# Keys of the first chunk transposed by TensorE instead of by DMA, with new stage priorities, in a two-layer attention and MLP kernel

## Chip, cores, metric

The kernel runs on one core of a Trainium2 chip. The metric is the device time of one execution in microseconds (us). An execution is called fast unless it fell in a slower state of the chip (lower TensorE clock throughout); all comparisons here are of fast runs. Engine names as in the profile: PE is TensorE (PEld its weight loads), ACT ScalarE, DVE VectorE, POOL GpSimd, SP SyncE, which issues most DMAs.

## The reference

Two layers over a sequence of 2048 rows of width 576: sliding-window attention, then an MLP, each behind a layer norm and with a residual.

```python
def _A_ref(x, wqkv, wo):                       # B, S, D = 1, 2048, 576
    H = 32; Dh = 18; W = 256
    q, k, v = ...  # (x @ wqkv) split into three and into heads
    scores = einsum("bhqd,bhkd->bhqk", q, k) * Dh ** -0.5
    mask = (i - j >= 0) & (i - j < W)
    p = softmax(where(mask, scores, -1e9))
    return (p @ v, heads joined) @ wo
def _B_ref(x, w1, b1, w2, b2):                 # inner width 4608
    return gelu(layernorm(x) @ w1 + b1) @ w2 + b2
x = A_x
for layer in range(2):                         # written out in the original
    x = x + _A_ref(layernorm(x), A_wqkv, A_wo)
    x = x + _B_ref(layernorm(x), B_w1, B_b1, B_w2, B_b2)
```

## The kernel before

The rows of each layer are cut into four chunks of 512, so there are eight chunks, 0 to 7. Attention of one chunk runs beside the MLP of the chunk before: ACT's exponentials leave PE time, and the matmuls of the second MLP product (hT times w2) fill it. I call those matmuls *filler*. A chunk's attention has 24 units (one group of four heads times one set of key blocks), in two stages of twelve (`ea`, `eb`); a unit is one group of score matmuls, two exponentials on ACT, masks on POOL, and 16 small matmuls with the values. The MLP of a chunk runs in two halves (`ga`, `gb`).

The order of instructions isn't written by hand. Each piece of work is a task with an estimated duration and a priority, and a planner places them one at a time, by the earliest possible start and then by priority:

```python
class Plan:
    def add(self, eng, fn, ..., cost=0.1, lat=0.1, prio=0.0, ...):
        stage = self.stage + ("+" if dma in ("w1", "w2", "xr") else "")
        prio += self.nudge.get(stage, 0.0)       # the annealed shift of this stage
        ...
    def schedule(self):
        ...
                    key = (round(st, 3), t.prio, t.idx)   # st: earliest start by the plan's costs
```

In the first 140 us the planner also puts warm-up matmuls into holes that it foresees on PE. The priorities, `PL.nudge`, hold one shift for each stage and were found by annealing, a search that changes them at random and mostly keeps what helps.

The queries and keys of a chunk come out of the projection as rows in PSUM, are cast to bf16 by DVE and ACT (`qn`), and have to be transposed, since the scores contract over the head dimension. Before, DMA did it, eight 128x128 blocks at a time:

```python
def qkv(k, i, prio0):                            # chunk k, row block i
    for n, w in enumerate("qkv"):
        bs = two_out(...)                        # projection on PE into two PSUM banks
        ...                                      # casts into qn by DVE and ACT
        dst, dn = ...                            # where the transposed block goes: qT or kT
        add("sp", lambda e, dst=dst, sl=sl: e.dma_start_transpose(dst, qn[:, sl, :]),
            reads=[f"qn{sl}h0", f"qn{sl}h1"], writes=[dn], dma="t", ...)
```

The softmax here doesn't subtract the row's maximum and nothing guards it: scores larger than these inputs give would overflow.

## Time and profile before

| | before |
|---|---|
| median of three runs | 934.0 us (932.31 to 935.26) |
| span of the profiled run | 932.2 us, mean PE clock 0.996 |
| PE busy | 900.0 us, 97% |
| PE idle from 0 to 100 us | 14.3 us |
| PE idle from 800 to 820 us | 3.25 us, clock 0.83 |

The prediction shows the lines behind this table. PE's matmuls of the MLP begin, in each half, with a group of six whose weights have 64 rows (a line reads `64*128 64x512`). The starts of the first such group of each half are good marks for comparing two kernels: 16 halves, the first at 100.1 us, then 149.6, and the last three at 764.5 (`ga` of chunk 6), 813.2 (`gb` of chunk 6) and 855.5 (`ga` of chunk 7), before a last half at 891.4. A half clock shows in the windows view at a fine grain. Its columns are the stretch, its length, busy time of PE, PEld, DVE, ACT and POOL, then the granted PE clock as a share of the full one, and two columns for DMA (its busy share and GB/s) that the argument doesn't use.

### The profile page before, as it was taken

What the parts mean: (1) busy time and instruction counts of PE and PEld (TensorE: products, weight loads), DVE (VectorE), ACT (ScalarE), POOL (GpSimd) and SP (SyncE); (2) the same over time, 40 slices, a digit from 0 to 9 for tenths busy, and PEclk for the clock granted to TensorE, in tenths of its full rate; (3) what the DMA queues carried; (4) which work ended last, traced back from release to release, by engine and by line L of the source; (5) the groups of instructions that cost most, each with busy time, mean ns of one, the idle gap of its engine ahead of it and who ended that gap; (6) DMA issues with size and microseconds to landing.
All of it is one profiled execution on the core that took longest, in us unless ns stands there. A gap on an engine that the chain in (4) does not pass through costs nothing. (4 is left out here: it accounts for less than half of the span.)

```text
span 932.2 us, 22378 instructions
## 1 busy us (share of the span) xinstructions
PE 900.0 (97%) x9343; PEld 566.3 (61%) x9382; DVE 320.0 (34%) x796; ACT 593.9 (64%) x717; POOL 372.8 (40%) x507
## 2 busy tenths in 40 slices
PE   8888999999999999999999999999999999899998
PEld 6555465655756657566565647577475665647556
DVE  5746222452238322174221812275022610232001
ACT  3687677767735777564677668636776677752541
POOL 3777444453504635054241635125452453500100
PEclk9999999999999999999999999999999999999999
DMA  9997839564295332964348351873619534345430
GB/s 212 137 248 123 201 95 259 130 156 124 47 242 118 116 115 28 240 139 140 113 66 253 66 191 40 215 147 63 198 39 234 137 119 144 113 121 148 160 115 26
DMA packets 225684, 130.06 MB, mean 140 GB/s; under 512 B 156080, under 2 KB 223408, under 8 KB 225584
## 3 DMA queue, kind: packets, MB, share of 16 engines
q1 hardware_dynamic: 216272, 120.95, 53.0%
q0 software_dynamic: 6880, 5.03, 4.1%
q10 hardware_dynamic: 2432, 2.65, 0.9%
q8 instruction: 74, 1.21, 0.6%
q14 instruction: 26, 0.21, 0.1%
HBM read 91.87 MB, written 2.36 MB: 101 GB/s over the span
## 5 line engine op out<-in xcount | busy, mean ns | idle before, releaser
L749 ACT ACTIVATE pT<-ps 128x1024 bf16<-128x1024 f32 (+2 forms) x384 | 347.9, 971 | 134.5 <-PE ps L740 133.2
L770 POOL TENSOR_SCALAR_AFFINE_SELECT pT<-pT 128x512 bf16<-128x512 bf16 (+1 forms) x368 | 282.0, 790 | 268.9 <-ACT pT L749 260.5
L904 PE MATMUL ps<-w_sb,hT 128*128 128x288 bf16 x2304 | 314.9, 286 | 1.3 <-DVE x_res L821 1.0
L878 ACT ACTIVATE hT<-ps,b1col 128x512 bf16<-128x512 f32 x288 | 198.0, 688 | 169.6 <-PE ps L875 169.6
L875 PE MATMUL ps<-xnTm,w_sb 128*128 128x512 bf16 x1113 | 259.4, 381 | 2.9 <-issue 1.2
L904 PEld LDWEIGHTS ps<-w_sb,hT 128*128 128x128 bf16 x2304 | 210.9, 97 | 73.5 <-issue 19.1
L875 PEld LDWEIGHTS ps<-xnTm,w_sb 128*128 128x128 bf16 x1152 | 109.4, 98 | 134.0 <-issue 17.7
L821 DVE TENSOR_TENSOR x_res<-ps,x_res 128x288 f32<-128x288 f32 x160 | 71.5, 449 | 244.5 <-PE ps L904 217.8
L670 PE MATMUL ps<-wqkv,xnTa 128*128 128x288 bf16 x960 | 135.8, 286 | 7.0 <-DVE qn L705 4.8
L670 PEld LDWEIGHTS ps<-wqkv,xnTa 128*128 128x128 bf16 x960 | 88.1, 98 | 44.4 <-DVE qn L705 10.0
L787 PEld LDWEIGHTS ps<-vA,pT 128*128 128x128 bf16 x2880 | 94.4, 96 | 27.5 <-POOL pT L770 11.0
L787 PE MATMUL ps<-vA,pT 128*128 128x20 bf16 x2880 | 100.7, 172 | 4.6 <-DVE attq L802 2.8
L705 DVE CAST qn<-ps 128x288 bf16<-128x288 f32 x120 | 54.5, 456 | 143.6 <-PE ps L670 141.1
L886 POOL TENSOR_TENSOR x_res<-x_res,b2bc 128x576 f32<-128x576 f32 x32 | 44.9, 1402 | 97.3 <-ACT hT L878 97.3
L740 PE MATMUL ps<-qT,kT 32*128 32x384 bf16 (+2 forms) x1216 | 64.1, 276 | 5.0 <-ACT pT L749 3.0
L602 POOL TENSOR_SCALAR vtmp<-mv_all 128x1 f32<-128x1 f32 (+1 forms) x43 | 8.4, 195 | 126.9 <-DVE mv_all L593 125.4
L591 DVE BATCH_NORM_STATS2 st_all<-x_res 128x6 f32<-128x288 f32 x104 | 44.6, 446 | 7.8 <-DMA x_res<-in_A_x_dram 6.6
L670 PE MATMUL ps<-wo_sb,attT 128*128 128x288 bf16 x320 | 45.4, 286 | 1.7 <-DVE x_res L821 1.7
L692 DVE CAST vA<-ps 128x288 bf16<-128x288 f32 x64 | 28.9, 454 | 50.6 <-PE ps L670 50.5
L863 PE MATMUL ps<-xnTm,w_sb 64*128 64x512 bf16 x288 | 40.2, 382 | 3.1 <-ACT pT L749 2.2
L797 DVE RECIPROCAL rinv<-ps 128x16 f32<-128x16 f32 x64 | 16.3, 255 | 76.6 <-PE ps L787 76.4
L740 PEld LDWEIGHTS ps<-qT,kT 32*128 32x128 bf16 x1216 | 19.5, 92 | 33.5 <-issue 19.2
(39 smaller groups left out, 290.9 us busy)
## 6 DMA issues: line engine op xcount, KB each, us to landing
w_sb<-in_B_w_dram SPq DMA_DIRECT2D x48, 864.0 KB, 6.2
w_sb<-in_B_w_dram SPq DMA_DIRECT2D x48, 768.0 KB, 4.8
w_sb<-in_B_w_dram SPq DMA_DIRECT2D x96, 48.0 KB, 4.5
x_res<-in_A_x_dram POOLq DMA_DIRECT2D x4, 1152.0 KB, 8.1
out_dram<-xn SPq DMA_DIRECT2D x16, 144.0 KB, 1.9
wqkv<-in_A_wqkv_dram ACTq DMA_DIRECT2D x3, 576.0 KB, 6.8
hT<-in_A_x_dram SPq DMA_DIRECT2D x2, 576.0 KB, 6.4
wo_sb<-in_A_wo_dram ACTq DMA_DIRECT2D x1, 576.0 KB, 6.6
```

The lines of the kernel that those rows point to most:

```text
L591: add("dve", lambda e, i=i, s=s: e.bn_stats(st_all[:, t, i, :], s[:, t, i * HB:(i + 1) * HB]), reads=res, writes=[f"st{t}_{i}"], cost=0.37 ...
L670: ins = e.matmul(bank(bs[o])[:, 0:HB], lhs(c), rhs(c, o * HB), start=(c == 0), stop=(c == KD - 1))
L705: add("dve", lambda e, b=bs[o], dst=dst: e.tensor_copy(dst, bank(b)[:, 0:HB].rearrange("p (h d) -> p h d", d=DH)), reads=[bs[o]], writes=[ ...
L740: ins = e.matmul(two(bs[j // 2])[:, j % 2, col:col + nq * 128], k_of(T0 + so)[0][32 * j:32 * j + 32, g, :], qs[32 * j:32 * j + 32, g, qo * ...
L749: add("act", lambda e, h2=h2: e.activation(pT[:, sl, 2 * h2:2 * h2 + 2, lo:hi], two(bs[h2])[:, :, lo:hi], ACT.Exp, scale=SCALE), reads=[bs ...
L770: add("pool", lambda e, ap=ap, pat=pat, sgn=sgn, kind=kind: e.affine_select(ap, ap, pattern=pat, compare_op=(ALU.is_ge if kind == "d" else ...
L787: ins = e.matmul(bank(B_O)[:, o:o + VW], pT[:, sl, j, col + qi * 128:col + (qi + 1) * 128], vA[:, (T0 + so) % VS, 4 * g + j, :], start=(fi ...
L821: add("dve", lambda e: e.tensor_tensor(x_res[:, t, sl], bank(b)[:, 0:HB], x_res[:, t, sl], ALU.add), reads=[b], writes=[f"x{t}h{hh}"], cos ...
L875: ins = e.matmul(bank(bk)[:, 0:n], w1_sb[:, sl, col:col + 128], xnTm[:, k % 2, c, 0:n], start=False, stop=(c == 3))
L878: add("act", lambda e, ff=ff, fl=fl, bk=bk: e.activation(hT[:, fl, 0:n], bank(bk)[:, 0:n], ACT.Gelu_apprx_tanh, bias=b1col[:, ff:ff + 1]), ...
L886: add("pool", lambda e, t=t: e.tensor_tensor(x_res[:, t, :], x_res[:, t, :], b2bc[:, :], ALU.add), reads=["b2", f"h{fl}"], writes=X(t), co ...
L904: ins = e.matmul(bank(b)[:, 0:HB], hT[:, fl, i * 128:(i + 1) * 128], w2_sb[:, fl, hh * HB:(hh + 1) * HB], start=(fl == 0), stop=(fl == NFH ...
```

## The change

The intent: keys of the first chunk should not wait in the DMA queue, where seven of the eight transposes of the chunk leave one after another behind a load of input rows. For the keys of chunk 0 alone, PE transposes the eight blocks into a PSUM bank and ACT copies the bank out. Since this shifts the load of each engine, the priorities were annealed again.

```diff
-    PL.nudge = {"ea0": -16.73, "q1.0": -5.72, "q1.1": -31.53, ...        # 53 stages
+    PL.nudge = {"": 0.63, "ld0+": 7.4, "q1.0": -16.88, "q1.1": 0.39, ... # 44 stages, none with the old value
...
+                if k == 0 and (w == "k"):
+                    b = Bank(FILL)
+                    def fn(e, b=b, sl=sl):
+                        ins = None
+                        for c in range(G):                                # G = 8
+                            ins = e.transpose(bank(b).bitcast(BF16)[:, c * 128:(c + 1) * 128],
+                                              qn[:, sl, c * 128:(c + 1) * 128], ident[:, :])
+                        return ins
+                    add("pe", fn, ..., cost=0.55, lat=0.22, prio=prio - 0.02, alloc=[b])
+                    src = bank_of(b)
+                    add("act", lambda e, dst=dst, src=src: e.copy(dst, src()), ..., cost=0.95, lat=0.17, prio=prio)
+                    continue
                 add("sp", lambda e, dst=dst, sl=sl: e.dma_start_transpose(dst, qn[:, sl, :]), ...
```

## The prediction

> **What bounds the kernel now.** I read the page's share of each engine first, then the list of engine busy times in 20 us windows, the chain of waits that ended last, and the timeline of the two stretches where the windows show TensorE (PE) idle.
>
> The page, engine totals:
> ```profile
> PE 900.0 (97%) x9343; PEld 566.3 (61%) x9382; DVE 320.0 (34%) x796; ACT 593.9 (64%) x717; POOL 372.8 (40%) x507
> ...
> PE 40%; DVE 2%; ACT 1%; issue 0%; DMA 0%; POOL 0%; DVEq 0%; POOLq 0%
> ```
> PE is busy 900.0 of 932.2 us, and the chain that ended last is PE work for nearly all that it could follow; DMA and ScalarE (ACT) have about 1% or less of it. So a change pays only by (a) taking away PE work, (b) taking away some of the 932.2 - 900.0 = 32.2 us of PE idle, or (c) taking away time in which PE ran at a lower clock. Windows (length, then busy PE, PEld, DVE, ACT, POOL, then the granted clock and DMA):
> ```profile
> 0.00:20.00 20.00, 17.66 (x135) 13.50 (x135) 10.61 (x30) 6.56 (x12) 7.54 (x23) 1.00 0.91 214
> 20.00:40.00 20.00, 16.40 (x207) 11.05 (x207) 14.39 (x44) 11.81 (x17) 11.86 (x16) 1.00 1.83 148
> 40.00:60.00 20.00, 16.70 (x246) 10.69 (x247) 10.89 (x27) 15.91 (x23) 15.53 (x23) 1.00 1.26 238
> 60.00:80.00 20.00, 17.01 (x285) 10.65 (x282) 8.04 (x20) 18.91 (x23) 15.44 (x21) 1.00 1.04 174
> 80.00:100.00 20.00, 17.97 (x271) 12.82 (x271) 16.74 (x45) 12.41 (x14) 12.98 (x23) 1.00 0.74 117
> 100.00:120.00 20.00, 19.68 (x115) 9.13 (x118) 1.17 (x3) 13.41 (x20) 6.22 (x6) 1.00 0.78 232
> ...
> 800.00:820.00 20.00, 16.75 (x221) 10.40 (x220) 3.45 (x9) 13.34 (x15) 9.53 (x13) 0.83 0.44 141
> ```
> The first 100 us hold 100 - 85.74 = 14.3 us of PE idle; the window at 800 holds 3.25 us more and is the only one in mid-kernel whose clock is under 1.00. From 100 to 800 the idle sums to about 11 us in 700. So there are two places to gain anything: the start, where chunk 0's keys are made, and one gap near 810.
>
> **The start.** Timeline of the kernel before (start, length, engine, line, what; in brackets the idle before it and its releaser):
> ```profile
> 13.17 3.60 SPq L712 DMA_TRANSPOSE kT<-qn  x1
> ...
> 18.79 1.18 DVE L591 BATCH_NORM_STATS2 st_all<-hT 128x6 f32<-128x288 bf16 x3 [1.63 <-DMA hT<-in_A_x_dram]
> ...
> 20.38 1.40 PE L670 MATMUL ps<-wqkv,xnTa 128*128 128x288 bf16 x10 [1.27 <-DVE qn L705]
> ...
> 22.14 0.34 PE L740 MATMUL ps<-qT,kT 32*128 32x384 bf16 x4 [0.36 <-DMA qT<-qn]
> ...
> 27.54 0.40 PE L740 MATMUL ps<-qT,kT 32*128 32x384 bf16 x8 [0.98 <-DMA kT<-qn]
> ...
> 27.98 4.39 ACT L749 ACTIVATE pT<-ps 128x1024 bf16<-128x1024 f32 x6 [3.94 <-PE ps L740]
> ```
> Eight DMA transposes (four of queries, four of keys) leave one queue in turn. The issue of the first key transpose takes 3.60 us, since a load of input rows stands before it. The first scores start at 22.14, the second, which need keys 1 and 3, only at 27.54, behind a key transpose. ACT idles 3.94 us for them. After that ACT runs the exponentials of chunk 0 and the first of chunk 1 until 80.1 with further waits of 1.26, 0.85, 2.36, 0.30, 0.38, 1.04, 0.75 and 0.24 us (7.2 in sum): this stretch goes at ACT's pace, not PE's.
>
> **The gap near 810.**
> ```profile
> 810.36 0.40 PE L740 MATMUL ps<-qT,kT 32*128 32x256 bf16 x8 [1.13 <-ACT pT L749]
> ...
> 813.20 1.46 PE L863 MATMUL ps<-xnTm,w_sb 64*128 64x512 bf16 x6 [1.89 <-ACT pT L749]
> ```
> At the end of the last attention chunk PE has run out of other matmuls: it waits 1.13 and 1.89 us for exponentials. The six matmuls then take 1.46 us where the same six take 0.82 elsewhere: half clock. The stretch from 813 to 819 has a mean clock of 0.53.
>
> **What the Trainium skill says.**
> 1. "TensorE: Matmul & The Clock Gate", Part 4: PE-mode transpose, gives about 275 ns for a 128x128 transpose within a kernel and says that the result lands in PSUM and has to be copied out. Five such transposes are in this trace (line L628): 219 ns each, but pipelined, ten in 0.89 us, so 0.089 us apiece.
> 2. "VectorE: DVE Perf Modes", The three transpose paths, gives 1309 ns for the DMA transpose of one 128x128 block. The key transposes here carry eight blocks, hold the queue for a median of 1.28 us and land after a median of 3.3 us, up to 9.4. So latency, not throughput, is what the change can remove.
> 3. "ScalarE: Activation LUTs", What ACT_TABLE_LOAD costs: 186 ns + 0.833 ns per element with immediate scale and bias, which for 1024 elements is 1.04 us. The trace agrees: exponentials over 1024 elements take 1025 ns and the copies of 640 elements 694 (formula: 719).
> 4. "TensorE: Matmul & The Clock Gate", Why this matters for your kernels, warns of PE idle gaps of more than about 3 us because of the clock. Here 1.13 + 1.89 us, parted by one short group, were followed by the half clock, so the trace agrees roughly.
>
> **The change, part by part.**
> *Removed:* four DMA transposes from the queue, at least 4 x 1.28 = 5.1 us of issue time between 13 and 26 us, and the latency of keys. The three later query transposes move up. Also three of 50 warm-up matmuls, 0.3 us.
> *Added on PE:* 4 x 8 transposes x 0.089 = 2.85 us, all before the second scores. PE is idle 1.27 + 0.36 + 0.98 us and more in that stretch, so they fit in idle time; if the exponentials still set the pace until 80 us, this costs nothing.
> *Added on ACT:* four copies of 1024 elements, about 0.97 each pipelined = 3.9 us. The order of instructions of the changed kernel puts two before the first exponential, where ACT idles 0.7 to 0.8 us between its casts, and two between the first and second unit, in the place of the 3.94 us wait. So not free, but hidden.
> *First scores:* they need queries 0 to 2. In the kernel before, queries 1 and 2 held the queue from 16.87 to 19.90; with the first key gone, query 1 takes the stalled slot (ends about 17), query 2 ends about 18.5. They could land 1.5 us earlier. But the changed order has VectorE (DVE) start the row statistics after the fifth cast, not the sixth. In the kernel before those statistics waited 1.63 us for the input rows, till 18.79, holding up the next cast. That wait now stands before the cast of query 3, so PE gets its next PSUM bank about 20.1, and the first scores come about 20.9: 1.2 us gained.
> *Second scores:* DVE has then statistics between the casts of keys 2 and 3; I add 1.4 us of them, the cast (0.46), next ones, the cast of key 3 about 24.0, 8 transposes 0.7, a copy 1.0 and hand-overs 0.5: 26.2 in place of 27.54, 1.3 us gained.
> *Rest of the stream to 80 us:* the warm-up matmuls that the scheduler put in between 28 and 43 us are gone from there, so it plans for fewer holes; the 7.2 us of waits may shrink by some 0 to 2 us. I take 0.7. Start in all: 2.0 us.
> *Moved: the priorities.* In the kernel before, the last two units of the last attention chunk have no filler between their scores (matmuls of the second MLP product); total filler for those twelve units is 144 matmuls in both kernels. The changed order has 6 to 18 of these between all scores, and 6 after the last. Estimate for the gap: PE time per unit is 12 x 0.123 + 0.49 (values) + 0.34 (scores) = 2.3 us against 1.94 for ACT's two exponentials, so PE can stay the slower engine to the end. At the very end it must wait for the last two exponentials (1.94 + 0.2) with 0.49 + 0.74 + 0.49 = 1.7 us of work, so 0.4 us of idle remains of 3.0: 2.6 gained. The half clock cost: from 813.20 to 822.36 is 9.2 us for work that at full clock is 0.82 + 23 x 0.22 + 0.5 + 0.5, about 6.9 with its small gaps: 2.3 us. I give 75% that it goes: 1.7. Sum 4.3.
> *Other gaps:* 0.57 us at 198, 0.80 at 416, 1.46 at 517, 0.3 to 0.4 at 635 and 656 are all places where the order changes. I expect no more than 0.5 us either way and count 0.
> Sum: 2.0 + 4.3 = 6.3 us. 934.0 - 6.3 = 927.7 us, 0.7%.
>
> **The rivals.**
> *The start gives nothing, or costs.* The transposes take three shared PSUM banks longer than a product does (about 0.7 + 0.2 + 1.0 us until the copy is done, against 0.61 + 0.2 + 0.46), and their copies stand in ACT's order ahead of casts. If PE waits for banks at every transpose, the first scores gain nothing and 2.85 us of PE work are added: 934.0 + 1 - 4.3, about 931. For it: PE already waits 1.27 us for a bank there. Against: the query latency is relieved too.
> *The gap stays or moves.* The new priorities came from a cost model whose start I can't test; a hole of the same kind elsewhere would give back the 4.3: about 932.
> *The whole stream of exponentials tightens.* If the start goes to ACT's floor, 3.94 + 7.2 us of waits less about 4 us of added copies and some hand-over leaves up to 5 us gained in the start, with 5 at the gap: 924.
>
> **Range and chances.** The central sum gives 927.7; the rivals lie at 931 to 932 on one side and 924 on the other, so 8 in 10: 923.8 to 931.5. Faster by over 2% would mean 18.7 us, more than all idle of the first 100 us (14.3) plus anything likely at the gap: 0.01. Slower by over 2% would need a new stall of that size: 0.01. Within 2%: 0.98.
>
> **What would show it.** Right: first scores about 21 us, second about 26; ACT's wait before the second unit of exponentials under 2.5 us, with two copies in it; PE idle in the first 100 us about 9.5 (2 us of time and 2.5 us of added work taken from 14.3); no window after 100 us with a clock under 1.00 except at the end; the last attention chunk going into the MLP with under 1 us of PE idle. Wrong: a wait of PE for DVE or ACT banks of over 2 us between 15 and 26; second scores at 27 or later; a clock under 0.9 anywhere in the middle; or PE idle from 100 to 800 over 12 us.

## More of the kernel before

The kernel before, inside the gap near 810 us:

```profile
812.00:813.00 1.00, 0.00 (x0) 0.00 (x0) 0.00 (x0) 1.00 (x2) 0.97 (x2) 0.50 1.05 363
```

PE does nothing in this microsecond while ACT works through, and the clock has gone to 0.50. It stays there until 818.6, 5.4 us after the matmuls have begun again at 813.2.

## The result, and the profile after

| | before | after |
|---|---|---|
| median of four runs each, same chip | 933.73 us | 926.31 us |
| range | 932.31 to 935.26 | 925.0 to 926.71 |
| ratio, with 95% interval | | 0.9918 (0.9899 to 0.9937) |
| span of the profiled run, clock | 932.2 us, 0.996 | 924.9 us, 0.998 |

A ratio here is the mean time of one kernel's fast runs over the mean of the other's in the same rounds, so it isn't quite the ratio of the medians beside it. The result is 7.4 us (0.8%) less by medians; the prediction had said 6.3. The class "within 2%" and the range were right.

Engine totals and shares of the chain that ended last, kernel after:

```profile
PE 900.4 (97%) x9374; PEld 566.6 (61%) x9411; DVE 320.2 (35%) x796; ACT 598.2 (65%) x721; POOL 373.7 (40%) x507
...
PE 70%; DMA 3%; issue 2%; DVE 2%; POOL 2%; ACT 1%; POOLq 0%
```

PE still sets the end and has about as much work as before; ACT has 4.3 us more, the four copies. What shrank is the rest of the span: 924.9 - 900.4 = 24.5 us of PE idle where there were 32.2. The windows of 20 us of the kernel after, with columns as above:

```profile
0.00:20.00 20.00, 17.75 (x146) 13.29 (x147) 11.17 (x33) 8.38 (x13) 7.53 (x23) 1.00 0.87 213
20.00:40.00 20.00, 18.05 (x231) 12.26 (x228) 13.73 (x44) 15.81 (x22) 13.95 (x19) 0.91 1.05 107
40.00:60.00 20.00, 18.15 (x282) 11.32 (x280) 9.97 (x24) 17.33 (x24) 15.59 (x23) 1.00 1.30 264
60.00:80.00 20.00, 18.90 (x299) 12.93 (x297) 11.42 (x32) 16.31 (x20) 15.45 (x23) 1.00 0.80 127
80.00:100.00 20.00, 17.58 (x251) 11.73 (x245) 13.61 (x33) 13.73 (x15) 12.81 (x19) 1.00 0.69 139
...
800.00:820.00 20.00, 19.17 (x212) 10.84 (x211) 2.44 (x7) 15.95 (x20) 7.54 (x10) 1.00 0.72 198
```

The first five rows add to 90.43 us of busy PE, so 9.57 us of idle where 14.3 were. The stretch at 800 is now at full clock with 0.83 us of idle. New is a clock of 0.91 between 20 and 40 us, to which one experiment below is given.

The start of the kernel after, from the timeline (start, length, engine, line, what; in brackets the idle before it and its releaser):

```profile
13.79 0.61 PE L721 MATMUL ps<-ident,qn 128*128 128x128 bf16 x8
...
14.43 1.01 ACT L725 COPY kT<-ps 128x1024 bf16<-128x1024 bf16 x1
...
17.75 0.82 DVE L590 BATCH_NORM_STATS2 st_all<-hT 128x6 f32<-128x288 bf16 x2 [0.96 <-DMA hT<-in_A_x_dram]
...
18.98 0.79 PE L669 MATMUL ps<-wqkv,xnTa 128*128 128x288 bf16 x5 [0.41 <-DVE qn L708]
...
19.70 0.34 PE L755 MATMUL ps<-qT,kT 32*128 32x384 bf16 x4
...
22.46 2.07 ACT L725 COPY kT<-ps 128x1024 bf16<-128x1024 bf16 x2
...
24.68 0.40 PE L755 MATMUL ps<-qT,kT 32*128 32x384 bf16 x8
...
25.13 1.94 ACT L764 ACTIVATE pT<-ps 128x1024 bf16<-128x1024 f32 x2 [0.59 <-PE ps L755]
```

Each of these lines answers to one of the kernel before in the prediction. The key transposes are the `ident,qn` groups, eight in 0.61 us. The first scores start at 19.70 (22.14 before), the second at 24.68 (27.54). Neither waits for a DMA any more, and ACT's wait ahead of the second unit's exponentials is 0.59 us, not 3.94, with two copies of keys in the time that it used to idle.

The end of the last attention stage, kernel after:

```profile
806.37 0.90 PE L919 MATMUL ps<-w_sb,hT 128*128 128x288 bf16 x6
807.87 0.55 PE L802 MATMUL ps<-vA,pT 128*128 128x20 bf16 x16 [0.61 <-POOL pT L785]
808.35 0.82 PE L878 MATMUL ps<-xnTm,w_sb 64*128 64x512 bf16 x6
```

There is filler (`w_sb,hT`) right up to the end, one wait of 0.61 us where there were 1.13 and 1.89, and the first six matmuls of the MLP take 0.82 us, not 1.46: full clock.

**Where the 7.3 us of the two profiled spans came from**, by the marks described above:

| stretch | before | after | less by |
|---|---|---|---|
| start to the first MLP half | 100.1 | 96.7 | 3.4 |
| from there to `ga` of chunk 6 | 664.4 | 663.9 | 0.5 |
| last attention stage, to `gb` of chunk 6 | 48.7 | 47.8 | 0.9 |
| from there to the next half | 42.3 | 39.8 | 2.5 |
| the rest | 76.7 | 76.7 | 0 |

The marks alone mislead a little near the end, since the orders differ in what lies between them: after has two more groups of 16 value matmuls (0.5 us each) in the stage and one fewer in the stretch after it. The windows of the stage, before and after (length, then busy PE):

```profile
764.50:813.20 48.70, 45.37 (x505) 27.57 (x508) 6.32 (x16) 37.83 (x45) 24.05 (x29) 0.99 0.44 141
...
760.60:808.35 47.75, 46.41 (x537) 27.85 (x539) 6.98 (x17) 37.82 (x45) 24.01 (x29) 1.00 0.40 127
```

So the stage had 48.70 - 45.37 = 3.33 us of idle before and 47.75 - 46.41 = 1.34 after, and 2.0 us of idle went. In the stretch after it, 2.5 us less 0.5 for the missing value group leaves 2.0 for the clock. The 0.5 us of the middle row is then the work that moved. So: 3.4 at the start, 2.0 + 2.0 at the end, about nothing in between. The part in between is also the least steady: it took 663.7 to 666.4 us in the five profiled runs with the order of the kernel after (its own among them), and 664.4 to 666.7 in the four with that of the kernel before.

### The profile page after: what moved, and what is told of

Same layout as the page of the kernel before. It is cut to its first block, busy times and chain, and to the rows that moved or that the text cites. A ratio compares the mean times of both kernels' runs of the same rounds, so it can differ in the third digit from the quotient of the medians.

```text
span 924.9 us, 22416 instructions
## 1 busy us (share of the span) xinstructions
PE 900.4 (97%) x9374; PEld 566.6 (61%) x9411; DVE 320.2 (35%) x796; ACT 598.2 (65%) x721; POOL 373.7 (40%) x507
## 4 chain that ended last, share of the span: by engine, by line
PE 70%; DMA 3%; issue 2%; DVE 2%; POOL 2%; ACT 1%; POOLq 0%
PE ps L919 25%; PE ps L890 21%; PE ps L669 11%; PE ps L802 6%; PE ps L755 4%; PE ps L878 3%; DMA xnTm<-xn 2%; POOL pT L785 1%; ACT pT L764 1%; DMA xnTa<-xn 1%; DVE xn L613 1%; DVE x_res L836 1%; POOL x_res L901 0%; DVE st_all L590 0%; DVE xn L618 0%
## 5 line engine op out<-in xcount | busy, mean ns | idle before, releaser
L890 PE MATMUL ps<-xnTm,w_sb 128*128 128x512 bf16 x1115 | 255.1, 379 | 3.5 <-issue 2.4
L919 PEld LDWEIGHTS ps<-w_sb,hT 128*128 128x128 bf16 x2304 | 211.4, 97 | 74.0 <-issue 18.5
L613 DVE TENSOR_SCALAR xn<-x_res,mv_all,rstd 128x576 bf16<-128x576 f32 x52 | 36.7, 709 | 14.8 <-DMA xnTm<-xn 9.6
```

The source lines that it names most:

```text
L613: add("dve", lambda e: e.tensor_scalar(xn[:, sl, 0:D], s[:, t, :], mv_all[:, t, 0:1], rstd[:, t:t + 1], op0=ALU.subtract, op1=ALU.mult), r ...
L890: ins = e.matmul(bank(bk)[:, 0:n], w1_sb[:, sl, col:col + 128], xnTm[:, k % 2, c, 0:n], start=False, stop=(c == 3))
L919: ins = e.matmul(bank(b)[:, 0:HB], hT[:, fl, i * 128:(i + 1) * 128], w2_sb[:, fl, hh * HB:(hh + 1) * HB], start=(fl == 0), stop=(fl == NFH ...
```

## The experiments

The theory after the first look: keys on PE give the start its 3.4 us, the new order gives the end its 4, and each of the two ends counts in full because PE, which sets the end, has no other slack there. Rivals: the priorities alone do it; the keys alone do it; the end is chance of the clock. Every run gave correct outputs. Where I write "frozen order", the planner ran as in the named kernel, and its order was edited afterwards.

All results, each with the ratio to the kernel before of the same rounds:

| run | median, us | before, us | ratio (95%) |
|---|---|---|---|
| order_only | 933.64 | 933.62 | 0.9998 (0.9983 to 1.0013) |
| after_dma | 929.83 | 933.62 | 0.9956 (0.9941 to 0.9971) |
| before_pe | 934.92 | 933.62 | 1.0017 (1.0001 to 1.0034) |
| after_hole | 931.73 | 933.62 | 0.9976 (0.9959 to 0.9992) |
| before_warm | 932.93 | 933.92 | 0.9979 (0.9967 to 0.9991) |
| after_warm | 926.6 | 933.92 | 0.9925 (0.991 to 0.9941) |
| before_nonudge | 955.19 | 933.92 | 1.0218 (1.0192 to 1.0244) |
| after_nonudge | 949.32 | 933.92 | 1.0165 (1.015 to 1.0179) |
| before_fill | 937.89 | 932.79 | 1.0054 (1.0029 to 1.0078) |
| after_twice | 927.67 | 932.79 | 0.994 (0.9916 to 0.9964) |
| before_fill2 | 931.17 | 932.06 | 0.9985 (0.9964 to 1.0007) |
| keys_only | 997.07 | 932.06 | 1.0696 (1.0666 to 1.0725) |

### order_only: the new priorities, keys still by DMA

```diff
 before, with
-    PL.nudge = {"ea0": -16.73, ...}     # of before
+    PL.nudge = {"": 0.63, ...}          # of after
```

> The kernel before with the new priorities alone; keys of the first chunk still transposed by DMA. From the fourth attention chunk on its TensorE order equals that of the changed kernel, the first 80 us stay near those of the kernel before. Theory (start and end each give a part): the end gap and its half clock go, the start gains nothing: about 929.5 us, 4 to 4.5 us under the kernel before, first GELU still near 101.9 us. Rival 1 (the priorities give all, the keys nothing): 926.3 us. Rival 2 (the keys give all): 933.5 us.

Measured: no change (0.9998), which is the number of rival 2 (the keys give all); but the trace shows a gain at the end, and a loss elsewhere. The scores, from the timeline of this run, wait for DMA as those of the kernel before do:

```profile
21.54 0.34 PE L739 MATMUL ps<-qT,kT 32*128 32x384 bf16 x4 [0.45 <-DMA qT<-qn]
...
26.96 0.40 PE L739 MATMUL ps<-qT,kT 32*128 32x384 bf16 x8 [1.01 <-DMA kT<-qn]
```

The first MLP half comes at 99.5 us, so the start gained 0.6 at most. The end did gain: 816.2 to 856.0 is 39.8 us, as in the kernel after. But the middle lost it again: from 99.5 to 768.4 is 668.9 us where before and after have 664.4 and 663.9, with 13.86 us of PE idle between 100 and 800 us (10.99 before). Of the 5.0 us more than in the kernel after, 3.6 arose before 321 us. A change of priorities makes the planner plan everything anew, and with DMA keys it finds other orders up to the sixth group of twelve units, which is in that stretch. What follows: the priorities alone pay nothing, and they are no part that can be undone by itself. So the next two runs keep an order fixed and change the keys alone.

### after_dma: the order of after, keys by DMA again

```diff
 after, frozen order:
-  PE: 8 transposes of the key block; ACT: copy of it
+  SP: dma_start_transpose of the key block, in the place of PE's transposes; ACT: nothing
```

> The changed kernel in its own order of instructions, frozen, with only the four key transposes and their copies put back to DMA transposes at the same places. Theory: first scores back near 22 us, second near 27.5 us, the later order unchanged: about 929.5 us, 3 us over the changed kernel, with no low clock near 810 us. Rival 1 (keys give nothing): 926.3 us. Rival 2 (keys give all): 933.5 us.

Measured: 929.83 us, as the theory said. The ratios 0.9956 and 0.9918 stand 0.38% apart, which is 3.5 us; the spans (928.0 and 924.9) 3.1. The timeline of this run:

```profile
19.16 0.79 PE L670 MATMUL ps<-wqkv,xnTa 128*128 128x288 bf16 x5 [1.76 <-DVE qn L728]
21.26 0.46 PE L777 MATMUL ps<-qT,kT 32*128 32x384 bf16 x4 [1.31 <-DMA qT<-qn]
...
28.87 0.40 PE L777 MATMUL ps<-qT,kT 32*128 32x384 bf16 x8 [2.00 <-DMA kT<-qn]
```

The three waits are back, and the scores come 1.6 and 4.2 us later than in the kernel after. At the first MLP half 2.6 us of that are left, at the last 3.1. So the keys, in this order, are worth about 3 us, and they get it at the start. (The order was not planned for DMA keys, so this is the worth within this order and not in the best order for each.)

### before_pe: the order of before, keys by PE

```diff
 before, frozen order:
-  SP: dma_start_transpose of the key block
+  PE: 8 transposes into PSUM bank 0 or 1; ACT: copy of it   # keys 2 and 3 behind the first exponentials
```

> The kernel before in its own order, frozen, with the four key DMA transposes replaced in place by eight TensorE transposes and a ScalarE copy each. Theory (the keys pay only in an order that moves the second scores up): in the old order 30 products stand before the second scores until 26.5 us, so at most the 1.0 us of waiting goes and 2.4 us of TensorE work is added: 932.5 to 934 us, half clock near 810 still there. Rival (the latency of the keys alone is worth its 3 us in any order): 930.5 us.

Measured: 934.92 us, nothing gained (1.0017), and 0.9 us over the range of the theory. The profiled run has its second scores at 27.07 us, only 0.5 earlier than the kernel before, and the first MLP half at 98.8, 1.3 earlier. By the half that begins at 586.73 (589.43 in the kernel before) it was 2.7 us ahead, but at the next one 1.0 behind. What it lost stands at 637 us, from the timeline of this run:

```profile
637.01 5.52 PE L671 MATMUL ps<-wqkv,xnTa 128*128 128x288 bf16 x30 [1.50 <-DMA xnTa<-xn]
```

PE waited 1.50 us for a DMA of normalized rows, and half clock followed, so that the 30 matmuls took 5.52 us where they take 3.83. The profiled run of the kernel before has no wait there, nor has before_fill2; before_warm, with the same order there, waited 1.17, so this wait varies from run to run. What follows: in the old order, where queries, casts and copies stand in the places that suited a DMA, the keys on PE bring a lead of 1.3 us at the first MLP half, and nothing of it shows in the time of six executions. Whether the wait at 637 us comes with the change or by chance isn't shown.

### keys_only: keys by PE, planned anew with the old priorities

```diff
 after, with
-    PL.nudge = {"": 0.63, ...}          # of after
+    PL.nudge = {"ea0": -16.73, ...}     # of before
```

> The changed kernel with the priorities of the kernel before: the keys on TensorE, the order planned anew with the old priorities. In the instruction order of this kernel several attention stages (the 5th, 11th and 16th groups of twelve units) have next to no projection matmuls left between their last scores, so the theory (order and keys pay only together) expects it clearly slower than the kernel before: 950 to 975 us, with waits of TensorE and low-clock windows in those stages. Rival (the keys give the gain whatever the priorities): 926 to 930 us.

Measured: 997.07 us, 65 us over the kernel before. The direction was expected and the size missed by over 20 us. From the timeline and the windows of this run:

```profile
19.87 0.34 PE L756 MATMUL ps<-qT,kT 32*128 32x384 bf16 x4
...
25.67 0.40 PE L756 MATMUL ps<-qT,kT 32*128 32x384 bf16 x8
...
201.38 6.75 PE L670 MATMUL ps<-wo_sb,attT 128*128 128x288 bf16 x35 [6.28 <-DMA attT<-attq]
```

```profile
200.00:220.00 20.00, 13.98 (x142) 8.30 (x146) 12.97 (x33) 9.48 (x10) 10.48 (x17) 0.68 0.43 86
...
860.00:880.00 20.00, 13.00 (x232) 6.74 (x230) 2.14 (x6) 17.55 (x19) 14.91 (x20) 0.54 0.14 51
```

The keys do what they should: scores at 19.87 and 25.67, about 2 us earlier than in the kernel before. It helps nothing, since the first MLP half is at 103.7, 3.6 us later than there, and further on whole stages have no filler left: PE waits 6.28 us for the transposes of an attention chunk, and in the stretch at 860 it runs at 0.54 of its clock. By the totals, PE idle is 995.5 - 919.8 = 75.7 us (32.2 before), and busy time grew from 900.0 to 919.8 with the same work, by the low clock: 43.5 + 19.8 = 63.3, the whole difference of the spans. The expectation named both waits and clock from the order of instructions, and took both far too small.

### before_nonudge and after_nonudge: no priorities at all

```diff
-    PL.nudge = {...}
+    PL.nudge = {}
```

> The kernel before with no priorities added at all (its scheduler's plain order). Not annealed, so slower than the kernel before: 936 to 948 us. It is the base for the next run.

> The changed kernel with no priorities added: from the sixth attention chunk on its TensorE order equals that of the run without priorities before. Theory (TensorE keys move the first and second scores up by about 2.5 us even in a plain order): 1 to 4 us under that run. Rival (the keys pay only through annealed priorities): within 1 us of it, or slower.

Measured: 955.19 us (950.15 to 959.23) and 949.32 us (948.11 to 951.89). Both expectations missed: the first is 7 us over its range, and the second is 5.9 us under the first, not 1 to 4. Annealing is worth some 20 us to either kernel, nearly three times the whole change. Without priorities the kernel with keys on PE is again ahead at the scores (20.16 and 25.14 against 21.85 and 27.21) and in the median. But the two profiled runs have equal spans (949.7 and 950.1), and the one with PE keys reached its first MLP half 5 us later. With a spread of 9 us between the executions of one kernel I take no size from this pair. Together with keys_only it shows that the earlier scores come with any order that is planned for keys on PE, and that the order decides whether they reach the end.

### after_hole: the old end put into the kernel after

```diff
 after, frozen order: the last 18 filler matmuls
-  between and behind the last two score groups of the last stage
+  ahead of the last but one score group
```

> The changed kernel with 24 filler matmuls of the last attention chunk moved from after its last but one scores to before them, so that the last two scores have no filler behind them as in the kernel before; everything else in place. Theory: TensorE waits 2 to 3 us more for exponentials there and the clock falls to half for some 3 us, so 929 to 931 us. Rival (order at the end is not what gave the gain): 926.3 us, within 0.5.

(The edit moves 18 matmuls, not 24: six of the 24 stood ahead of the last but one scores already.)

Measured: 931.73 us, 0.7 over the range of the theory; by ratios (0.9976 and 0.9918) 0.58% or 5.4 us over the kernel after. The gap is there again, in the timeline of this run:

```profile
810.09 0.40 PE L766 MATMUL ps<-qT,kT 32*128 32x256 bf16 x8 [0.64 <-ACT pT L775]
...
812.85 0.55 PE L813 MATMUL ps<-vA,pT 128*128 128x20 bf16 x16 [1.87 <-ACT pT L775]
...
814.49 1.49 PE L901 MATMUL ps<-xnTm,w_sb 128*128 128x512 bf16 x3 [0.33 <-issue]
```

Three matmuls take 1.49 us, at full clock 0.81. PE idle in the stage is 50.4 - 46.6 = 3.8 us (1.34 in the kernel after), and the stretch after it takes 41.3 us instead of 39.8. That is 2.5 + 1.5 = 4.0 us for the gap (0.55 of it a wait for DVE at 806.25, which the kernel after doesn't have); the rest of the difference of the profiled spans (931.4 - 924.9 = 6.5) arose between 97 and 763 us, where the order is the same as in the kernel after, and so isn't the gap's. This run shows by itself that where the filler stands, with the same work, is worth about 4 us.

### before_warm: the clock alone

```diff
 before, frozen order:
+  9 warm-up matmuls ahead of the last score group of the last stage
+  15 warm-up matmuls ahead of the MLP half behind it
```

> The kernel before with 9 and 15 dummy matmuls put into its two waits near 810 us, on a PSUM bank that is free there; nothing else moved. Theory (the half clock there is a second cost of the hole, apart from the idle time): no window near 815 us under full clock, the waits for exponentials stay, about 2.3 us gained: 931.4 us. Rival (the low clock is only a sign and costs nothing, or does not come from idle time): 933.7 us.

Measured: 932.93 us; 1.0 us less by medians, 0.21% or 2.0 us by ratios; between the theory and the rival. Windows view of this run:

```profile
800.00:820.00 20.00, 19.65 (x281) 13.60 (x280) 3.90 (x10) 15.59 (x18) 11.26 (x16) 1.00 0.42 135
```

PE's wait isn't shorter, only filled, and the clock is 1.00 throughout. From the MLP half to the next takes 40.1 us where the kernel before takes 42.3 for the same matmuls. So the half clock costs up to 2.2 us where it strikes, separately from the idle time. The profiled run is no faster than that of the kernel before (932.3 and 932.2 us), as it lost 1.0 us before the first MLP half and 1.3 between there and the last attention stage, where nothing was changed. Nor does the kernel before lose the same in each execution: its mean clock ranges from 0.993 to 0.998, and before_pe, with its order at this place, had 3.4 us of half clock there and not 6.8.

### after_warm: the half clock near 33 us

```diff
 after, frozen order:
+  4 and 6 warm-up matmuls into the hole of PE at 30 to 32 us
```

> The changed kernel with 4 and 6 dummy matmuls in its waits between 30 and 32 us, where its trace shows TensorE busy 0.74 of 2 us and then half clock from 33 to 37 us. Theory (the half clock at the start costs what five-matmul groups at 1.38 in place of 0.79 us show, about 1.2 us): 925.0 us and no window under full clock before 40 us. Rival (ScalarE sets the pace there, so it costs nothing): 926.3 us.

The kernel after has a half clock of its own. Windows of it:

```profile
30.00:32.00 2.00, 0.74 (x21) 0.39 (x17) 2.00 (x8) 1.25 (x2) 1.23 (x2) 1.00 3.28 79
...
34.00:36.00 2.00, 1.87 (x11) 0.70 (x10) 1.41 (x6) 1.22 (x4) 1.83 (x5) 0.50 0.91 84
```

With the hole filled the clock was 1.00 in this run from 20 to 40 us, and it changed nothing, as the rival said: 926.6 us (after: 926.31), first MLP half at 96.4 (96.7). PE at half clock is still fast enough there, as ACT's exponentials set the pace. This version doesn't beat the kernel after.

When does half clock come? The clock records of the thirteen fast traces answer it. Half clock starts and ends on a grid of 3.41 us: it runs from 33.29 to 36.70 in the kernel after (one cell of the grid) and from 811.79 to 818.62 in the kernel before (two). By PE's busy time in each cell at full clock, half clock followed 25 of the 26 cells that were busy for less than half, 10 of 25 between 0.50 and 0.62, and none of 3449 above. It ended after each of the 25 cells at half clock that were busy for over 0.85, and after none of the 16 under 0.80. So what counts is the busy share of a whole cell and not the longest wait, and one and the same hole can cost two cells, one or none, by how it lies on the grid.

### after_twice: the transposes on PE doubled

```diff
-                        for c in range(G):
+                        for c in list(range(G)) * 2:
```

> The changed kernel with each of the 32 key transposes issued twice, order otherwise frozen: 32 more TensorE transposes, at the 0.055 us apiece of its trace some 1.8 us more TensorE work before the second scores. Theory (this work lies in TensorE's idle time while the exponentials set the pace, so only what stands before the second scores is paid): second scores up to 1.5 us later, whole kernel 926.5 to 927.8 us. Rival (TensorE work at the start is paid in full): 928.1 us or more.

Measured: 927.67 us, by ratios (0.994 and 0.9918) 2.0 us over the kernel after, with overlapping intervals. The second scores of this run now wait for a copy:

```profile
25.60 0.40 PE L755 MATMUL ps<-qT,kT 32*128 32x384 bf16 x8 [0.29 <-ACT kT L725]
```

They are 0.9 us later, yet the first MLP half is at 96.7, as in the kernel after. So at the first MLP half nothing of the doubled transposes is left. The profiled run is 1.9 us longer than that of the kernel after, and all of it arose between 97 and 763 us (665.8 us against 663.9), where the order is the same and runs differ by up to 2.7 us. The 1.4 us of the medians are within what I can't tell apart here.

### before_fill and before_fill2: the old kernel with the gap filled

```diff
 before, frozen order: six groups of six filler matmuls of the last stage
-  where they stood
+  later, between the last four score groups
 before_fill2 only:
-  the three weight reloads that follow these groups, where they stood
+  later too, each behind the last group that reads the old weights
```

> The kernel before in its own order, frozen, with only the last 36 filler matmuls of the last attention chunk set a little later, so that each of its last four scores has 6 or 12 behind it and 6 stand after the last; keys still by DMA, start untouched. Theory (hole and half clock are a part of the gain of their own): TensorE waits under 1 us before the MLP, full clock near 815 us, first GELU still near 101.9: 929 to 931 us, 3 to 4.5 under the kernel before. Rival (the end costs only when the start is right, or the wait just moves): 933 us or more.

before_fill measured 937.89 us, but is a mistake of mine: the groups moved stood behind the reload of their own weights, so they waited for it and used the next half's weights. It says nothing on the question. (Its outputs still passed the comparison with the reference, which therefore doesn't notice a slip in so few products.) One execution, the profiled one (1125.39 us, mean clock 0.751), is left out everywhere.

> The kernel before, with six groups of six projection matmuls moved later, between the last four score groups of the last attention stage, and the three weight reloads that follow them moved with them. It mends before_fill, whose moved groups stood behind the reload of their own weights, and so waited for the next half's: a mistake of that edit. Theory: the hole of 1.13 + 1.89 us is filled without any added work, the wait ahead of the last MLP half of that stage is under 1 us, the clock stays full near 811 to 819 us, and the median is 929 to 931 us, 3 to 4.5 under the kernel before. Rival (the hole is paid elsewhere, since the groups moved are missing earlier): 933 us or more, with the wait moved to an earlier score group of the stage.

Timeline and windows of before_fill2:

```profile
812.94 0.82 PE L887 MATMUL ps<-xnTm,w_sb 64*128 64x512 bf16 x6 [0.89 <-ACT pT L773]
```

```profile
800.00:820.00 20.00, 18.09 (x237) 11.04 (x238) 3.52 (x9) 15.94 (x19) 10.07 (x14) 1.00 0.51 141
```

In the trace it does what the theory says: the last wait is under 1 us, the clock full, the stage 47.9 us (48.7 before) and the stretch after it 40.1 (42.3), 3.0 us in sum. The median, 931.17 us, falls in the theory's band, but the kernel before was itself quicker in these rounds (932.06, single runs from 930.05 to 935.31), so the gain is 0.9 us by medians and 0.15% or 1.4 us by ratios, with an interval that includes no change (1.0007). The rival's picture (the wait moved to an earlier group of the stage, 933 us or more) didn't come about either. So the mechanism at the end is shown; that it brings the whole 3 us in an average execution of the old kernel is not.

## Why the prediction was right

Time, range and class were right. By its own steps, predicted against measured:

| term | predicted gain, us | measured, us |
|---|---|---|
| start | 2.0 | 3.4 |
| idle in the gap near 810 | 2.6 | 2.0 |
| half clock after it | 1.7 | 2.0 |
| other gaps | 0 | about 0 |
| sum | 6.3 | 7.4 |

That the sum came so near is in part luck: errors of 1.4, -0.6 and 0.3 us.

**The start: mechanism right, size off by 1.4.** The prediction had "first scores come about 20.9" and the second at 26.2; they came at 19.70 and 24.68. Of the 3.4 us, 2.9 were there at the second scores (1.3 predicted) and 0.6 came in the stream after them (0.7 predicted). Two terms of the first scores were mis-sized. The prediction let query 1 take "the stalled slot (ends about 17)", but the stall didn't pass on to it: issued 1.3 us later, query 1 held the queue for 1.30 us and not 3.60, and query 2 ended at 17.5, not 18.5. In all fast traces the first transpose behind that load held the queue for 3.0 to 3.6 us where it was issued at once, and for 1.2 to 1.9 where it was issued about 1 us or more later; why isn't shown. And the prediction kept 18.79 for the start of the row statistics, which wait for that load; they started at 17.75, so PE's wait for the next cast was 0.41 us and not 1.27. This differs between runs of one order: before_warm and before_fill2, equal to the kernel before up to there, have it at 18.41 and 17.95. The transposes were smaller too, 8 in 0.61 us, of which the first takes 0.219: (0.61 - 0.219) / 7 = 0.056 us apiece, against 0.089 taken from a group of ten. The doubling run shows that this size hardly mattered. (The prediction speaks of five such transposes in the trace before; there are 20, in groups of five.) The copies took 1.01 us, two in 2.07, against the predicted 0.97 each, and were hidden as predicted. after_dma confirms the cause: without PE keys, in the same order, 3 us are lost, and the waits named in the prediction return. It takes the faster keys and the shorter queue for the queries back together; what each is worth isn't shown.

**The gap: both terms right in kind, and the sum near** (4.3 predicted, 4.0 measured). The prediction allowed 0.4 us of idle at the end; a wait of 0.61 us is left, with smaller ones in the stage. after_hole shows the worth by putting the gap back, before_warm separates the clock from the idle time. For the clock the prediction took 75% of 2.3 us; in the profiled pair it was 2.0.

**"Other gaps ... count 0" held**, but only for this order: order_only lost 4.5 us in just that middle part.

**The rivals.** "The start gives nothing" fell: PE didn't wait at each transpose. "The gap stays or moves" fell in the kernel after, though order_only and keys_only show that it was a real danger. "The whole stream of exponentials tightens" was in part true: of its up to 5 us, 3.4 came, but only 0.6 of them in the stream itself. Of the checks listed at the end of the prediction, both scores came 1.3 us before the times it gave. The others were met: ACT's wait 0.59 us with two copies ahead of it, 9.57 us of idle in the first 100 (about 9.5 predicted), no clock under 1.00 in a window of 20 us after 100 us until the end, 10.44 us of idle from 100 to 800. The 9.5 is luck in part: by the prediction's own terms it is 14.3 - 2 - 2.5 = 9.8, and its 2 us were 3.4. The half clock at 33 us it didn't foresee.

**What the prediction lacked.** It treated the two parts as a sum: keys for the start, priorities for the end. Within the order of the kernel after that holds: undone one at a time, the keys are worth 3.1 us of profiled span and the place of the filler 4.0, of 7.3. But the two edits of the program don't add. Priorities alone gave 0, keys alone in the old order 0, keys alone planned anew with the old priorities lost 65 us; together they gave 7.4. Why the annealed priorities are so sharp (a new order for the whole kernel when one early task changes) follows from how the planner picks tasks; which of the early choices spread to the sixth group and beyond I didn't trace. Also open is why no-priority kernels spread over 9 us.

## What to carry to other kernels

A transpose by DMA that others wait for cost its place in the queue here (3.60 us behind a load) more than its own time (1.28 us); on an engine that is idle just then it was nearly free, and the gain is read from the waits that name the DMA, if the order lets the work behind them move up. When an order comes from a planner, test each part within a frozen order, since planning anew changes everything at once, and priorities tuned for one kernel can be much worse than none for its neighbour. In a kernel bound by TensorE look for the place where filler runs out at a stage's end: what stands there can cost its idle time again in clock (2.0 and 2.0 us here), and the same matmuls placed later mend both.

## What the Trainium skill lacked or had wrong

- "TensorE: Matmul & The Clock Gate", Part 4: PE-mode transpose, gives about 275 ns for one transpose in a kernel's context. That section lacks the cost of several in a row (the page has one for ordinary matmuls only): here eight 128x128 transposes took 0.61 us, about 0.056 us apiece after the first.
- The same section says that transposes don't make the clock go to full speed. No run here bears that out or refutes it; they ran amid other matmuls at full clock.
- The same page, Why this matters for your kernels, warns of idle gaps of more than about 3 us. That row doesn't cover several shorter waits: here 1.13 and 1.89 us with 0.95 us of short matmuls between them gave half clock, and so did a stretch with 0.74 us of busy PE in 2 us. The page gives no share of busy time at which half clock comes; in these traces it came after 35 of the 51 cells of 3.41 us that were busy for less than 0.62, and after none above. The row also doesn't say that half clock may cost nothing: at 33 us, with ACT setting the pace, taking it away changed the time by nothing measurable (926.6 against 926.31 us).
- "VectorE: DVE Perf Modes", The three transpose paths, gives 1309 ns for the DMA transpose of one 128x128 block. That section lacks what a queue adds: here the 30 key transposes of eight blocks in the kernel before held the queue for 1.28 us in the median, and 3.60 us behind a load, and landed after 3.3 us in the median.
